# A spectral filter and a SiLU network on one core: rows of a transfer over more ports, loads of d2 two pieces ahead, roundings of the ramp at other places

## The chip, the cores and the metric

The kernel runs on one core of a Trainium2 chip. The metric is device time in microseconds (us) of one execution. Before the change it is 2659.55 us, the median of three runs (2658.20 to 2661.21).

A core has a matrix engine (TensorE, PE in the profile, with its weight loads as PEld), a vector engine (VectorE, DVE), a scalar engine (ScalarE, ACT), a general one (GpSimd, POOL), and SyncE (SP), which does nothing but issue transfers and wait. ACT and POOL issue transfers too. All transfers are moved by the core's 16 DMA engines. Each engine works through its own list of instructions in order and waits on semaphores where it needs another's result. SBUF is the on-chip memory of 128 partitions that engines and transfers use; PSUM holds the results of matmuls.

## What is computed

Two blocks, one after the other. The first filters a sequence in the frequency domain; the second is a small network on every token.

```python
# x: (8, 3008, 256), filt_r and filt_i: (1505, 256)
X = np.fft.rfft(x, axis=1)
F = (filt_r + 1j * filt_i)[None, :, :]
y = np.fft.irfft(X * F, n=x.shape[1], axis=1)
t = y.reshape(8 * 3008, 256)
h = t @ w_in                        # (256, 2048), given in float64
g = h * (1.0 / (1.0 + np.exp(-h)))
out = g @ w_out                     # (2048, 256), given in float64
```

## The kernel before

**The network.** It is the larger part. The 24064 tokens are cut into 48 pairs of chunks (`PAIRS`: two chunks of 256, 256 or 240 tokens), six pairs to one of the eight batch entries, here called blocks. A pair takes eight steps, one for each two slices of 128 hidden units, so a block has `STEPS` = 48 steps. In a step, `hidden` computes h and SiLU and `project`, one step behind, multiplies by w_out. Both products are done in seven instead of eight block products (the names A11, S1 to S4 and so on), which costs additions on DVE and POOL. A step has eight rounds (`ROUNDS`); after each one, pieces of other work whose due time has come are emitted. A due time is a step and a round, and `put(step, round, piece)` notes it. The order written out this way is the order in every engine's list.

**The filter.** The transform of length 3008 = 47 x 64 is done as matmuls in two stages, once forward and once back, with a pass through DRAM between the stages to exchange rows and columns:

- `load_x` brings pieces u = 0 to 7 of a block's input into SBUF. Of the 128 partitions, rows 0 to 46 (h = 0) and 64 to 110 (h = 1) are filled. A piece is loaded by four transfers: for each h one of 32 rows and one of 15. Blocks 0 and 1 use it for all pieces, the later ones for pieces 6 and 7 alone (the others come by `load_fold`). In block 0 even pieces are issued by SP and odd ones by ACT, and the unused rows 32 to 63 are zeroed first by a memset (L271), which the transfers that touch rows from 32 on wait for. `sums` (L291) adds and subtracts the two halves of the piece on DVE.
- `stage1` is the first matmul stage (L308). Its results are copied out by `evac`, which takes DVE and ACT by turns, and are written to d1 in DRAM from POOL (L313).
- `load_t2(g)` reads d1 back for groups g = 0 to 5 (L382). `forward` (L393) multiplies, `multiply` (L405) applies the filter on DVE, `add` (L413, L414) finishes the complex product, on POOL in block 0 and on DVE later.
- `inverse` (L426), `even` (L437) and `rows` (L445, L450) do the first stage back and write d2 in DRAM.
- `load_t4(g)` reads d2 for g = 0 to 7 (L455, two transfers on SP, into two buffers by turns). `stage3(g)` (L458) issues the load of piece g + 1, does 64 small matmuls (L469) and copies the result into y, the input of the network. In the steady part a block's pieces 0 to 3 are due 11, 9, 6 and 3 steps before the block's first step, pieces 4 to 7 at 10 3/8, 11 3/8, 16 3/8 and 18 6/8.

The filters stay in SBUF. `load_filters` (L219) fetches them in two parts, rows 0 to 3 of each partition (groups 0 and 1) and rows 4 to 11 (groups 2 to 5). Each part is 16 transfers, and each of these fills 16 neighbouring partitions: which frequency a partition holds follows from `kept`, from which the tables of the transform are built too.

**The weights.** They come as float64, and `load_weights` fetches the raw words of two slices by four transfers on SP. `round_weights(j)` makes float32 of slice j: five operations on DVE (L722 to L730), two on ACT, two products on POOL (L735), and after every second slice four more additions on POOL (`combine_weights`, L551).

**The ramp.** Before step 0 block 0 must go through the filter, and some weights must be there. The list at the end of the kernel sets that order: x loads, d_t, weights(0), first filters, `sums` and `stage1`, load_t2(0) and (1), e_t, rounded(0) and (1). Then for each group: forward; in group 0 the second filters, wi_t and wq_t; weights(1 + g) for g < 3; multiply and add; a rounding of slice g for g = 2, 3 and 4; and inverse_rows of the group before. After the last group come weights(4), load_t4(0), the roundings 5 to 8 (weights(5) after the first) and stage3(0) to (3). Then the steps begin, with the roundings 9 to 15 and block 1's x pieces 0 to 7 in their rounds; the x pieces 0 and 1 of block 1 and the first `tokens` and `sums` are due just before step 0.

**Transfers on SP and ACT** take eight completion semaphores by turns, as the kernel is built: the one that takes a semaphore waits until the transfer that had it before has landed. So at most eight transfers of the two are in flight. Those from POOL have eight of their own.

Of the kernel before, what the change touches and what calls it, by code (L numbers as in the profile page):

```python
# [52 lines left out]
B, S, C = 8, 3008, 256  # L53
DFF = 2048
N1, N2 = 47, 64
NS, NG = 24, 6
# [18 lines left out]
def slot_residue(g, bank, j):  # L75

    s = 2 * g + bank
    return (s, 47 - s, s + 12, 35 - s)[j]
# [6 lines left out]

def kept(sp):

    r = np.arange(32)
    return np.where(r < 16, sp + 94 * r, 94 * (r - 15) - sp)


def dft_tables():
# [63 lines left out]
def kernel(  # L156
# [47 lines left out]
    f_t = [cpool.tile([128, NG, 2, C], FP32, name=f"filt{i}") for i in range(2)]  # L204
# [5 lines left out]
    x_t = [x_all[:, i] for i in range(2)]  # L210

    def load_filters(first, last):
        for j in range(4):
            s0, tau = slot_residue(0, 0, j), (1 if j % 2 == 0 else -1)
            for half in range(2):
                off, t = (s0, tau) if half == 0 else (94 - s0, -tau)
                for k, filt in enumerate((filt_r, filt_i)):
                    p0 = 32 * j + 16 * half
                    nc.sync.dma_start(  # L219
                        out=f_t[k][p0:p0 + 16].rearrange("p g k c -> p (g k) c")[:, first:last],  # L220
                        in_=bass.AP(tensor=filt.tensor, offset=filt.offset + (off + t * first) * C,
                                    ap=[[94 * C, 16], [t * C, last - first], [1, C]]))

# [12 lines left out]
    def bank(b, name, spare=None):  # L236


        if b > 0 and spare is not None:
            return accps.tile([128, 2, C], FP32, name=name, tag=f"a{spare}")  # L240
        if b > 0 or early[0] is None:
            return fps.tile([128, 2, C], FP32, name=name, tag="f")
        early[0] += 1
        k = early[0] % 6
        if k < 2:
            return fps.tile([128, 2, C], FP32, name=name, tag="f")
        return accps.tile([128, 2, C], FP32, name=name, tag=f"a{k - 2}")

    def spectral(b):
# [3 lines left out]
        xs, us, t2s, banks, prods, halves, t4s = {}, {}, {}, {}, {}, {}, {}  # L253

        def load_x(u):


            queue = nc.sync
            if b == 0:
                queue = (nc.sync, nc.scalar)[u % 2]  # L260
                if u == 0:
                    us["t1"] = gpool.tile([128, 2, 2, 2, C], FP32, name="t1_g", tag="g")
                if u in (0, 2):
                    xs["y"] = ypool.tile([128, 2, HALF], FP32, name=f"x_{b}_{u}", tag="y")
                if u < 4:
                    xs[u] = xs["y"][:, u % 2, 0:1024].rearrange("p (a n) -> p a n", a=2)
                elif u < 6:
                    xs[u] = t4pool.tile([128, 2, 2 * C], FP32, name=f"x_{b}_{u}", tag="t4")
                else:
                    xs[u] = x_t[u % 2]  # L270
                (nc.vector, nc.gpsimd)[u % 2].memset(xs[u][32:64], 0.0)  # L271
            else:
                xs[u] = x_t[u % 2]
            for h in range(2):
                for r0, nr in ((0, 32), (32, N1 - 32)):
                    queue.dma_start(
                        out=xs[u][64 * h + r0:64 * h + r0 + nr],
                        in_=bass.AP(tensor=x.tensor,
                                    offset=x.offset + (b * S + 32 * r0 + 4 * u + 2 * h) * C,
                                    ap=[[32 * C, nr], [32 * N1 * C, 2], [1, 2 * C]]))  # L280

        def sums(u):
            if b > 0 or u % 3 == 0:
# [168 lines left out]
        def load_t4(g):  # L452
            t4s[g] = t4pool.tile([128, 4, C], FP32, name=f"t4_{b}_{g}", tag="t4")
            for h in range(2):
                nc.sync.dma_start(out=t4s[g][64 * h:64 * h + 2 * NS],  # L455
                                  in_=d2[:, 4 * g:4 * g + 4, h, :])

        def stage3(g):  # L458
            half, n0 = divmod(4 * g, 16)
            if g < 7:  # L460
                load_t4(g + 1)
            ps = [bank(b, f"pd_{b}_{g}_{h}").rearrange("p a c -> p (a c)")[:, 0:8 * N1]
                  .rearrange("p (a i n) -> p a i n", a=2, i=4) for h in range(2)]
            for cb in range(2):
                for i in range(4):
                    for c0 in (0, 64):
                        for h in range(2):
                            rows = slice(64 * h, 64 * h + 2 * NS)
                            nc.tensor.matmul(  # L469
                                out=ps[h][c0:c0 + 64, cb, i, :],  # L470
                                lhsT=t4s[g][rows, i, 128 * cb + c0:128 * cb + c0 + 64],
                                rhs=wi_t[rows, :], start=True, stop=True)
            if n0 == 0:
                y[b, half] = ypool.tile([128, 2, HALF], FP32, name=f"y_{b}_{half}", tag="y")
            dst = y[b, half].rearrange("p a (r h n) -> p a h n r", h=2, n=16)
            for h in range(2):
                evac(dst[:, :, h, n0:n0 + 4], ps[h])
# [7 lines left out]
    def put(step, rnd, piece, *args):  # L485

        pending.append((step + rnd / ROUNDS, len(pending), lambda: piece(*args)))

    def plan(b, part):

        at = STEPS * b
# [37 lines left out]
        for g, step in ((0, -32), (2, -24), (4, -16)):  # L529
# [3 lines left out]
            put(at + step + 1, 5, part["rows"], g, 0, 2)  # L533
            put(at + step + 2, 3, part["rows"], g, 1, 2)
        put(at - 14, 5, part["load_t4"], 0)
        for g, step in enumerate((-11, -9, -6, -3)):
            put(at + step, 3, part["stage3"], g)
        plan_rest(b, part)
# [219 lines left out]
    def weights(jp):  # L758
        if wide:
            load_weights(jp)  # L760

    def rounded(j):
        if wide:
            round_weights(j)
        else:
            load_exact(j)

    def inverse_rows(part, g):
        part["inverse"](g)
        for i in range(2):  # L770
            part["even"](g, i)
            part["rows"](g, i)
# [5 lines left out]
    part = spectral(0)  # L778
# [16 lines left out]
    for g in range(NG):  # L795
        part["forward"](g)
        if g == 0:
            load_filters(4, 2 * NG)
            nc.sync.dma_start(out=wi_t, in_=wi_dram.ap())
            nc.sync.dma_start(out=wq_t, in_=wq_dram.ap())  # L800
        if g < 3:
            weights(1 + g)
        for k in range(2):
            part["multiply"](g, k)
        for k in range(2):
            part["add"](g, k)
        if 2 <= g < NG - 1:
            rounded(g)
        if g > 0:
            inverse_rows(part, g - 1)  # L810
    inverse_rows(part, NG - 1)
    weights(4)
    part["load_t4"](0)
    for j in range(5, 9):
        rounded(j)
        if j == 5:
            weights(5)
# [4 lines left out]
    for b in range(1, B):  # L822
        plan(b, spectral(b))
# [67 lines left out]
```

## Time and profile before

The profiled execution took 2658.93 us, of which the span from the first to the last instruction is 2657.1. The profile shows for each engine when it worked and what ended its idle time.

| stretch (us) | what it is | PE busy | DVE busy | DMA share | GB/s |
|---|---|---|---|---|---|
| 0 to 20 | x loads, first stage | 11.93 | 14.61 | 0.71 | 198 |
| 20 to 40 | weights(0), first filters, d1 | 7.15 | 10.14 | 0.95 | 316 |
| 40 to 60 | groups 0 and 1, second filters | 8.11 | 6.66 | 0.96 | 182 |
| 60 to 80 | groups 2 and 3 | 7.86 | 14.33 | 1.03 | 249 |
| 80 to 100 | groups 4 and 5 | 15.28 | 16.40 | 0.54 | 165 |
| 100 to 130 | roundings 5 to 8, stage3, first step | 14.39 | 23.58 | 0.67 | 158 |
| 130 to 160 | first steps | 27.98 | 24.54 | 0.35 | 99 |
| 320 to 600 | steady part, for comparison | 279.89 | 187.05 | 0.28 | 69 |

"Busy" is the time in which the engine worked within the stretch, "DMA share" the mean busy share of the 16 DMA engines (a little over 1 where the records of packets overlap), and GB/s what they moved. A wait in a timeline stands in square brackets behind an instruction: how long its engine was idle before it and what ended that.

The first step's first matmul starts at 122.66 us. The clock that TensorE was granted is 1.00 until about 53 us, 0.50 from there to about 135 us, and 1.00 again from then on but for one stretch of 3.4 us near 222 us. Over the whole span PE is busy 97% of the time, DVE 65%, ACT 41% and POOL 18%.

### The profile page before, as it was taken

The numbers are of one execution on the slowest core, as the hardware profiler recorded it, in microseconds if no ns is written. First come the engines' busy times: TensorE is split into PE (matmuls) and PEld (weight loads), VectorE is DVE, ScalarE is ACT, GpSimd is POOL, SyncE is SP. The second block draws the span as 40 slices with busy tenths as digits, with TensorE's granted clock in tenths as the row PEclk, the third lists the DMA queues.
The fourth block names the chain that finished last, engine by engine and source line by source line (L and its number), as shares of the span: only waits on it lengthen the run. The fifth ranks groups of instructions, "written<-read, shape, count | busy, mean of one in ns | idle before, by whom it ended". The sixth has DMA issues, their size and how long they took to land.

```text
span 2657.1 us, 48172 instructions
## 1 busy us (share of the span) xinstructions
PE 2566.0 (97%) x18720; PEld 2166.4 (82%) x18720; DVE 1728.3 (65%) x3590; ACT 1095.7 (41%) x3000; POOL 484.1 (18%) x726
## 2 busy tenths in 40 slices
PE   4689999999999999999999999999999999999998
PEld 1368888888887888888888888888888788888987
DVE  5786766667666666666666676666766666555554
ACT  1244444443444444444444444444444444444443
POOL 4541111311121112112111211131112111100100
PEclk9599999999999999999999999999999999999999
DMA  8632221232223222231222322123222321111000
GB/s 229 176 103 64 75 67 45 70 78 71 50 72 80 55 63 73 69 70 48 75 64 56 70 75 67 44 70 77 71 50 72 79 56 28 48 22 27 9 16 16
DMA packets 206379, 176.11 MB, mean 66 GB/s; under 512 B 122916, under 2 KB 177956, under 8 KB 205748
## 3 DMA queue, kind: packets, MB, share of 16 engines
q1 hardware_dynamic: 185184, 120.90, 19.9%
q0 software_dynamic: 17296, 47.47, 5.6%
q10 hardware_dynamic: 3672, 4.67, 0.6%
q8 instruction: 147, 2.41, 0.4%
q14 instruction: 80, 0.66, 0.1%
HBM read 97.97 MB, written 84.41 MB: 69 GB/s over the span
## 4 chain that ended last, share of the span: by engine, by line
PE 90%; DMA 3%; DVE 3%; SPq 1%; issue 1%; ACT 1%; POOL 0%; ACTq 0%; DVEq 0%; POOLq 0%
PE acc L639 41%; PE px L580 25%; PE pyz L580 18%; PE pd L469 2%; DMA t<-d 2%; PE pb L393 2%; PE pc L426 2%; DVE g L551 1%; SPq L677 1%; PE pf L363 1%; PE pa L308 1%; DVE u L291 0%; DMA x<-in_x_dram 0%; DMA filt<-in_filt_r_dram 0%; DMA e_t<-e_tbl 0%
## 5 line engine op out<-in xcount | busy, mean ns | idle before, releaser
L639 PE MATMUL acc<-g,w_t 128*128 128x256 f32 (+1 forms) x5376 | 1513.8, 375 | 0.4 <-DVE g L551 0.4
L639 PEld LDWEIGHTS acc<-g,w_t 128*128 128x128 f32 x5376 | 1022.5, 190 | 116.1 <-DVE g L551 0.8
L551 DVE TENSOR_TENSOR g<-pyz,abc 128x256 f32<-128x256 f32 (+1 forms) x1152 | 480.0, 417 | 536.7 <-ACT abc L601 294.6
L551 DVE TENSOR_TENSOR g<-g 128x256 f32<-128x256 f32 (+3 forms) x1152 | 619.7, 538 | 196.7 <-ACT g L584 183.5
L580 PE MATMUL px<-ty,w_t 128*128 128x256 f32 (+1 forms) x2304 | 688.6, 381 | 3.5 <-ACT abc L595 3.0
L584 ACT ACTIVATE g<-g 128x256 f32<-128x256 f32 (+1 forms) x1152 | 473.0, 411 | 247.6 <-DVE g L551 247.5
L551 POOL TENSOR_TENSOR s<-s 128x256 f32<-128x256 f32 (+1 forms) x329 | 259.8, 806 | 1461.1 <-DVE s L657 1450.1
L580 PEld LDWEIGHTS px<-ty,w_t 128*128 128x128 f32 x2304 | 425.0, 190 | 88.5 <-issue 30.7
L580 PE MATMUL pyz<-y,w_t 128*128 128x256 f32 (+1 forms) x1536 | 454.7, 378 | 1.9 <-DVE g L551 1.9
L580 PEld LDWEIGHTS pyz<-y,w_t 128*128 128x128 f32 x1536 | 284.1, 190 | 48.4 <-DVE g L551 6.6
L595 ACT COPY abc<-px 128x256 f32<-128x256 f32 (+1 forms) x384 | 141.3, 368 | 365.8 <-PE px L580 365.8
L584 ACT ACTIVATE g<-px 128x256 f32<-128x256 f32 (+1 forms) x384 | 145.8, 380 | 308.8 <-PE px L580 308.8
L601 ACT COPY abc<-px 128x256 f32<-128x256 f32 (+1 forms) x384 | 143.7, 374 | 311.4 <-PE px L580 311.2
L580 PE MATMUL px<-y,w_t 128*128 128x256 f32 (+1 forms) x768 | 230.2, 382 | 3.6 <-ACT g L584 2.6
L580 PE MATMUL pyz<-ty,w_t 128*128 128x256 f32 (+1 forms) x768 | 225.9, 376 | 0.7 <-DVE g L551 0.7
L580 PEld LDWEIGHTS px<-y,w_t 128*128 128x128 f32 x768 | 142.1, 190 | 43.0 <-ACT g L584 15.4
L580 PEld LDWEIGHTS pyz<-ty,w_t 128*128 128x128 f32 x768 | 145.7, 190 | 18.6 <-DVE g L551 2.3
L588 ACT COPY abc<-px 128x256 f32<-128x256 f32 (+1 forms) x384 | 135.0, 352 | 2.7 <-PE px L580 1.3
L229 DVE COPY y<-pd 128x376 f32<-128x376 f32 x64 | 51.1, 804 | 112.2 <-PE pd L469 112.2
L469 PEld LDWEIGHTS pd<-wi_t,t 48*64 48x64 f32 x4096 | 71.2, 140 | 45.3 <-issue 32.3
L469 PE MATMUL pd<-wi_t,t 48*64 48x47 f32 x4096 | 80.3, 239 | 23.4 <-DMA t<-d 15.3
L393 PE MATMUL pb<-t,d_t 64*32 64x256 f32 x1536 | 61.7, 408 | 36.7 <-DMA t<-d 36.7
(67 smaller groups left out, 1346.0 us busy)
## 6 DMA issues: line engine op xcount, KB each, us to landing
t<-d SPq DMA_DIRECT2D x96, 256.0 KB
t<-d SPq DMA_DIRECT2D x128, 192.0 KB
d<-q POOLq DMA_DIRECT2D x85, 256.0 KB, 2.6
out_dram<-o SPq DMA_DIRECT2D x636, 32.0 KB
d<-tf POOLq DMA_DIRECT2D x144, 96.0 KB, 2.5
d<-t POOLq DMA_DIRECT2D x52, 192.0 KB, 3.1
xr<-in_x_dram SPq DMA_DIRECT2D x6, 1472.0 KB
x_all<-in_x_dram SPq DMA_DIRECT2D x72, 96.0 KB
```

Source lines behind the costliest of these rows:

```text
L229: nc.vector.tensor_copy(out=dst, in_=src)
L308: nc.tensor.matmul(out=ps[h][64 * par:64 * par + 64], lhsT=wf_t[rows, par], rhs=ut[rows, par], start=True, stop=True)
L393: nc.tensor.matmul(out=ps[k][32 * j:32 * j + 32, ri, :], lhsT=d_t[rows, 4 * g + at, ri, :], rhs=t2[rows, at, :], start=True, stop=True)
L426: nc.tensor.matmul(out=ps[j][64 * k:64 * k + 64, a, :], lhsT=e_t[rows, g + a, k, ri, :], rhs=zs[k][rows, ri, :], start=(a == 0 and ri == 0 ...
L469: nc.tensor.matmul(out=ps[h][c0:c0 + 64, cb, i, :], lhsT=t4s[g][rows, i, 128 * cb + c0:128 * cb + c0 + 64], rhs=wi_t[rows, :], start=True, ...
L551: eng.tensor_tensor(out=out, in0=in0, in1=in1, op=op)
L580: nc.tensor.matmul(out=out, lhsT=w_t[:, c, 0, jp], rhs=rhs, start=start, stop=True, skip_group_check=True)
L584: nc.scalar.activation(out=g[:, k, 0:n], in_=g[:, k, 0:n] if src is None else src, func=AFT.Silu)
L588: nc.scalar.copy(out=sums[:, 0, 0:n], in_=xo)
L595: nc.scalar.copy(out=sums[:, 1, 0:n], in_=xo)
L601: nc.scalar.copy(out=sums[:, 2, 0:n], in_=xo)
L639: nc.tensor.matmul(out=acc[pair][i][:, h, 0:n], lhsT=w_t[:, c, 1, jp], rhs=g[:, k, 0:n], start=(jp == 0 and h == 0), stop=last, skip_group ...
```

## The change

It has four parts.

- **Filters.** `kept` puts the frequencies of a residue on even partitions and those of its mirror on odd ones, where they were on the first and second 16 of a block of 32. So a filter transfer fills 16 partitions two apart, spread over 32, instead of 16 neighbours. The blocks of 32 are loaded in the order 0, 2, 1, 3. The tables follow `kept` by themselves; sizes and the number of transfers stay.
- **x rows.** A piece's 47 rows of one h are loaded by three transfers of 16, 16 and 15 rows that are three apart, instead of one of 32 and one of 15. Six transfers per piece instead of four. Each next transfer goes to the other h; odd pieces begin with h = 1. All transfers with h = 0 now touch rows from 32 on.
- **Loads of d2.** load_t4(1) is issued with load_t4(0), and stage3(g) issues load_t4(g + 2) after its matmuls instead of load_t4(g + 1) before them.
- **Roundings of the ramp.** Slices 2 and 3 are rounded after group 1, that is before group 2 is multiplied; slice 4 after the last group with 5 to 8. Before, slices 2, 3 and 4 were rounded within groups 2, 3 and 4.

```diff
 def kept(sp):
-    r = np.arange(32)
-    return np.where(r < 16, sp + 94 * r, 94 * (r - 15) - sp)
+    r = np.arange(32) // 2
+    return np.where(np.arange(32) % 2 == 0, sp + 94 * r, 94 * (r + 1) - sp)
...
     def load_filters(first, last):
-        for j in range(4):
+        for j in (0, 2, 1, 3):
...
-                    p0 = 32 * j + 16 * half
                     nc.sync.dma_start(
-                        out=f_t[k][p0:p0 + 16].rearrange("p g k c -> p (g k) c")[:, first:last],
+                        out=f_t[k][32 * j + half:32 * j + 32:2].rearrange("p g k c -> p (g k) c")[:, first:last],
...
-            for h in range(2):
-                for r0, nr in ((0, 32), (32, N1 - 32)):
+            for r0 in range(3):
+                for h in (range(2) if u % 2 == 0 else (1, 0)):
                     queue.dma_start(
-                        out=xs[u][64 * h + r0:64 * h + r0 + nr],
+                        out=xs[u][64 * h + r0:64 * h + N1:3],
                         in_=bass.AP(tensor=x.tensor,
                                     offset=x.offset + (b * S + 32 * r0 + 4 * u + 2 * h) * C,
-                                    ap=[[32 * C, nr], [32 * N1 * C, 2], [1, 2 * C]]))
+                                    ap=[[3 * 32 * C, (N1 + 2 - r0) // 3], [32 * N1 * C, 2], [1, 2 * C]]))
...
         def stage3(g):
-            if g < 7:
-                load_t4(g + 1)
...
+            if g < 6:
+                load_t4(g + 2)
...
         put(at - 14, 5, part["load_t4"], 0)
+        put(at - 14, 5, part["load_t4"], 1)
...
-        if 2 <= g < NG - 1:
-            rounded(g)
         if g > 0:
             inverse_rows(part, g - 1)
+        if g == 1:
+            rounded(2)
+            rounded(3)
     inverse_rows(part, NG - 1)
     weights(4)
     part["load_t4"](0)
-    for j in range(5, 9):
+    part["load_t4"](1)
+    for j in range(4, 9):
         rounded(j)
```

## Prediction, made before the changed kernel was run

> **What bounds the kernel now.** I read the page's busy shares first, then the windows over three stretches, then the waits, and last the timelines of the places that the waits name. The windows:
>
> ```profile
> 0.00:130.00 130.00, 64.71 (x715) 29.49 (x716) 85.71 (x140) 27.64 (x50) 60.39 (x85) 0.70 0.80 207
> 130.00:190.00 60.00, 52.95 (x236) 36.84 (x236) 51.19 (x93) 26.68 (x66) 29.96 (x41) 0.96 0.38 107
> 190.00:2657.00 2467.00, 2448.34 (x17771) 2100.06 (x17770) 1591.38 (x3358) 1041.42 (x2884) 393.78 (x601) 1.00 0.23 58
> ```
>
> From 190 us on the matmuls are busy for 2448 of 2467 us: TensorE sets the end, and only what leaves it idle can be won. The first 125 us, the ramp, are another kernel: PE is half idle, and the transfers (share 0.80) and the order on DVE set the pace. In the steady part one wait is left (the waits of PE, 190 us to the end):
>
> ```profile
> PE pd L469 <- DMA t<-d: 7.8, 12, 1.2
> ```
>
> Its place, in the timeline of the first block:
>
> ```profile
> 210.69 4.93 SPq L677 DMA_DIRECT2D out_dram<-o  x8
> ...
> 215.72 0.87 SPq L455 DMA_DIRECT2D t<-d  x2
> ...
> 219.02 0.28 PE L469 MATMUL pd<-wi_t,t 48*64 48x47 f32 x2 [1.04 <-DMA t<-d]
> 219.78 1.47 PE L469 MATMUL pd<-wi_t,t 48*64 48x47 f32 x62 [0.48 <-DMA t<-d]
> ```
>
> The load for stage3(5) stands on SP behind eight output stores and lands after PE wants it. The same happens once in each of the eight blocks. In the ramp the long wait is DVE's for the filters of groups 2 to 5, with the weights' rounding behind it:
>
> ```profile
> 63.63 0.69 DVE L405 TENSOR_TENSOR z<-pb,filt 128x512 f32<-128x512 f32 x1 [13.95 <-DMA filt<-in_filt_r_dram]
> ...
> 66.60 0.43 DVE L722 TENSOR_SCALAR work<-raw 128x512 uint32<-128x512 uint32 x1 [0.24 <-DMA raw<-in_moe_w_out_dram]
> ```
>
> and in the windows of that stretch the engines of the DMA are full while little moves:
>
> ```profile
> 52.00:56.00 4.00, 0.00 (x0) 0.00 (x0) 0.00 (x0) 0.00 (x0) 0.00 (x0) 0.65 0.66 137
> 56.00:60.00 4.00, 0.00 (x0) 0.00 (x0) 0.00 (x0) 0.00 (x0) 0.00 (x0) 0.50 1.16 121
> 60.00:64.00 4.00, 0.00 (x0) 0.00 (x0) 0.37 (x1) 0.00 (x0) 0.00 (x0) 0.50 1.09 113
> ```
>
> **What the Trainium skill says.** "SBUF — State Buffer", section Door 1: the port of a partition follows from its number; 16 neighbouring partitions reach 4 ports (104 GB/s), 32 reach 8 (189 GB/s), and +64 goes to the other eight. The trace agrees with the first: 113 to 121 GB/s at a full share above. "DMA: Bandwidth & Descriptors", anatomy of one DMA: some 2 us of each transfer do not depend on its size. Agrees: the page has 2.5 us to landing for 96 KB of tf and 2.6 for 256 KB of q; the first x transfers take 2.2 to 3.2 from issue to their last completion update. "TensorE: Matmul & The Clock Gate", part 1: an idle stretch halves the clock in steps of 3.4 us. Agrees: after the gap at 218 us the granted clock is 0.50 from 220.4 for 3.4 us. "SBUF — State Buffer", who interferes with whom: tensor_scalar and GpSimd lock each other out. Agrees: L724 takes 0.42 us alone and 0.95 beside POOL.
>
> **Steady part: d2's loads two ahead.** load_t4(5) now goes out after stage3(3), 13 steps before its use, instead of at stage3(4), one step before. Take the time from the start of the last matmul before a stage3 piece to the first after it: 1.39 us where nothing waits; in the eight stage3(5) 3.57, 1.80, 3.25, 2.02, 2.86, 2.08, 3.47, 2.92. Sum 21.97 - 8 x 1.39 = 10.85 us. In the first block the clock is also lost for 3.4 us at half: 1.7. Together 12.5 us off PE, which is the bound there. What is late next: the load behind the stores at step 10 is now load_t4(6), used 6 steps (some 40 us) later: nothing. New wait: SP now holds each load until stage3(g) has read the buffer; behind it stand stores and prefetches used steps later. Nothing, at most 1 us over the run. The twelve x transfers of pieces 6 and 7 per block instead of eight (0.4 us each on SP) are needed 1.6 steps later: nothing.
>
> **Ramp, x loads.** 32 transfers of 128 and 60 KB become 48 of 64 or 60. SP and ACT take eight completion semaphores in turn, so a transfer waits for the one eight before (the waits of SP, 0 to 20 us):
>
> ```profile
> SPq L276 <- DMA x<-in_x_dram: 5.8, 8, 1.3
> ```
>
> Before: last issue at 15.31, (15.31 - 0.91) / 31 = 0.46 us each, a life of 8 x 0.46 = 3.7. The ports of a whole half (47 rows) do not change; alternating halves relieve them. I take a life of 2.9 (between 2.3 alone and 3.7): 0.36 each, last issue 0.9 + 47 x 0.36 = 17.8, 2.5 later, and ACT's first eviction, which waits 13.57 us behind its issues, with it. Row 0 also waits for the memset on SP, 0.9 us. The first filters run faster behind it, so I take +1.5 us at load_t2(0) (ends -2 and +4).
>
> **Ramp, filters.** Sixteen transfers of 128 KB, first issue 42.46. The chain shows the last issued at 56.53 and landing 7.81 later, 64.34; the last eight landed about 1.1 us apart. On eight ports I take 0.55 us (ends 0.45 and 0.8; 189 GB/s of the page gives 0.68 as an estimate, alternating halves less). The first cannot land before t2(2), 48.9 + 1.5 = 50.4, so the last lands at 50.4 + 15 x 0.55 = 58.7, not 64.3.
>
> **Ramp, roundings.** Now rounded(2) and (3) stand before multiply(2) on DVE and need raw(1), which is behind the filters on SP. Before, raw's first half came 2.2 us after the filters (66.51 against 64.34): 60.9. One rounding with POOL free is 2.9 us (99.47 to 102.36), with POOL busy 4.4 (106.72 to 111.19); I take 6.5 for both: multiply(2) starts at 67.4, not 63.63. Then three roundings are gone from between the groups: 66.6-70.0, 75.64-79.33, 84.2-88.38, 11.3 us of the 35.9 from 63.63 to the last rows (99.56), which leaves 24.6. But on POOL the additions of group 2 now stand behind rounded(3)'s products and combine (1.4 + 2.9, up to 6): inverse(2) and rows(2) wait some 2.8 more. Rows end at 67.4 + 24.6 + 2.8 = 94.8. The tail has five roundings instead of four: 2.9 + 4 x 4.4 = 20.5 (before 16.1), end 115.3, as against 115.65. After it, before, PE waited for its loads:
>
> ```profile
> 118.69 0.41 PE L469 MATMUL pd<-wi_t,t 48*64 48x47 f32 x2 [2.98 <-DMA t<-d]
> 119.74 1.95 PE L469 MATMUL pd<-wi_t,t 48*64 48x47 f32 x62 [0.64 <-DMA t<-d]
> ...
> 124.54 1.28 DVE L291 TENSOR_TENSOR u<-x_all 111x512 f32<-111x512 f32 x2
> 125.74 0.42 DVE L551 TENSOR_TENSOR g<-pyz,abc 128x256 f32<-128x256 f32 x1
> ```
>
> With loads two ahead stage3(3) waits only for its banks: one eviction (0.8) and 2.0 us of matmuls, done at 118.1 instead of 121.7. But load_t4(5) now waits on SP for those matmuls, and block 1's first x loads stand behind it: 0.9 us of issue for load_t4(5), 2.6 for six x transfers, 2.8 to land: 124.4, where DVE could take them at 121. So u runs 124.4 to 125.6, and g at 125.6 against 125.74. Sum of the ramp: -0.1 us. The filters' gain is paid to the x loads, to POOL's order and to this wait. Ends: filters 0.45, no x loss and no POOL delay -6; filters 0.8 and +4 in front +6.
>
> **Sum.** -12.5 - 0.1 and 0.6 for small SP waits: -12.0. The profiled execution took 2658.93 (span 2657.1), so 2646.9; it lies 0.62 below the median 2659.55, which gives 2647.5.
>
> **Rivals.** (1) As summed, 0.62: 2643.5 to 2651.5. (2) The spread pays in full, the x of block 1 comes in time, 0.15: ramp -6, 2641.5. For it: 0.5 us per transfer is within what 16 engines moved at 24 to 32 us (around 400 GB/s); against: raw(1) still comes last. (3) More, smaller x transfers keep their life of 3.7 (48 x 0.46 = 22 instead of 15 us), 0.15: ramp +7.5, 2655. For it: the eight in flight. Half of it is within 0.2%. (4) Slower, 0.08: transfers to partitions two or three apart are themselves slower than to neighbours. Place: the second filters. The time to g is the filters' landing + 66.9, so the loss eats the 12.5 when they land at 71.3: (71.3 - 50.4) / 15 = 1.4 us per transfer, against 1.1 before. At 2.0 it would be +9, 2668. No row of this trace has such a stride; against it, each row stays a run of 1 to 8 KB. (5) That stage3(5) still waits: the order on SP excludes it.
>
> **Chances.** What a measurement of this kernel tells from no change is 0.2%, 5.3 us. Faster: cases 1 and 2 and a third of 3, 0.82; same 0.11; slower 0.07. The range 2640 to 2657 leaves out case 4 and the edges of 2 and 3, under 0.2.
>
> **What would show it.** PE's wait for t<-d after 190 us gone and no half clock at 220; eight stage3(5) at 1.39 us; the windows between 46 and 60 us at about 200 GB/s; multiply(2) on DVE after two roundings near 67, g's first addition near 125; a wait of u for x_all just before it. I am wrong if the filters land after 62, if ACT's first eviction starts past 20, or if DVE's waits for raw grow beyond the filters' gain.

## The result, and the profile after

The changed kernel takes 2660.26 us (median of four runs, 2659.17 to 2661.77); the kernel before took 2658.88 beside it. The ratio is 1.0005, with a 95% interval of 0.9988 to 1.0022: no change that can be measured. The forecast was 2647.5, so 12 us of gain are missing. The profiled execution of the changed kernel took 2659.17 us with a span of 2657.4 (before: 2658.93 and 2657.1).

The windows of the changed kernel over the three stretches of the prediction (columns: stretch, its length, busy us of PE, PEld, DVE, ACT and POOL with the number of instructions, granted clock, DMA share, GB/s):

```profile
0.00:130.00 130.00, 56.87 (x710) 26.56 (x710) 79.22 (x131) 25.26 (x45) 58.05 (x83) 0.76 0.72 204
130.00:190.00 60.00, 48.94 (x213) 33.52 (x214) 50.33 (x91) 25.59 (x64) 29.93 (x40) 0.90 0.41 114
190.00:2657.00 2467.00, 2453.15 (x17798) 2102.80 (x17797) 1595.45 (x3369) 1045.41 (x2892) 394.67 (x603) 1.00 0.23 58
```

In the first 190 us PE is busy 11.9 us less than before (105.8 against 117.7): the ramp has become longer. After 190 us it is busy for 2453 us instead of 2448, with 27 matmuls more. That is work left over from the late ramp, not a better filled engine. The waits of PE after 190 us say why the steady part won so little (engine, tile and line, what it waited for: us in total, times, longest):

```profile
PE pb L394 <- DMA t<-d: 3.5, 6, 1.1
```

Before, the tile here was pd (stage3), with 7.8 us. That wait is gone, and forward, which waited nowhere after 190 us before, has taken its place. The time from the last matmul ahead of a piece to the first after it counts more than the wait itself, since it holds the whole stall. Over 1.33 us, which a forward takes without a wait, the seven forward(0) of blocks 1 to 7 lose 1.78, 0.14, 2.10, 1.17, 0, 0.96 and 0.22: 6.36 us.

The place, a block after the one that the prediction showed. First the timeline of SP in the changed kernel (start, length, queue, line, operation, out<-in, how many):

```profile
853.73 4.58 SPq L679 DMA_DIRECT2D out_dram<-o  x8
858.66 2.71 SPq L383 DMA_DIRECT2D t<-d  x4
```

and that of PE in the same kernel:

```profile
854.73 1.15 PE L468 MATMUL pd<-wi_t,t 48*64 48x47 f32 x64
...
862.45 0.59 PE L394 MATMUL pb<-t,d_t 64*32 64x256 f32 x2 [0.31 <-DMA t<-d]
864.17 1.09 PE L394 MATMUL pb<-t,d_t 64*32 64x256 f32 x30 [1.13 <-DMA t<-d]
```

The same place in the kernel before, SP and then PE:

```profile
853.62 3.30 SPq L382 DMA_DIRECT2D t<-d  x4
```

```profile
851.61 0.28 PE L469 MATMUL pd<-wi_t,t 48*64 48x47 f32 x2 [0.93 <-DMA t<-d]
852.48 1.14 PE L469 MATMUL pd<-wi_t,t 48*64 48x47 f32 x62 [0.59 <-DMA t<-d]
859.82 1.09 PE L393 MATMUL pb<-t,d_t 64*32 64x256 f32 x32
```

In step 10 of a block, results are stored by two groups of eight transfers. The load for stage3(5) stood on SP behind the first eight, and the load for forward(0) stands behind all 16. Before, it landed at 858.49 (last completion update of load_t2(0)'s two transfers) and PE came at 859.82: 1.3 us of slack, because PE had just lost 1.9 us at stage3(5). In the changed kernel PE no longer loses them, while the load lands 5.5 us after its issue: 864.13. Seen from PE's step, the loads behind the stores are no earlier than before, and PE meets them one piece later.

The ramp, by when steps start (first of the 14 matmuls of `hidden` in the step), and the sum over the whole span:

| | before | after | difference |
|---|---|---|---|
| step 0 | 122.66 | 124.84 | +2.2 |
| step 1 | 131.62 | 138.19 | +6.6 |
| step 6 | 177.69 | 183.65 | +6.0 |
| stage3(5), eight places, over 1.39 us | 10.85 | 0 | -10.85 |
| clock at half near 222 us (in step 11) | 1.3 | 0 | -1.3 |
| forward(0), seven places, over 1.33 us | 0 | 6.36 | +6.36 |
| step 6 and the three rows below it, added | | | +0.2 |
| span | 2657.1 | 2657.4 | +0.3 |

The clock's share is worked out from the difference to before, which falls from +6.01 at the start of step 11 to +2.53 at the start of step 12: 3.48, of which 2.18 are that block's stage3(5). This share isn't shown to be the change's. All six kernels below that keep the old loads of d2 (e4, e7, e8, e9, e11 and e12) wait at the same stage3(5) and still have the full clock there. In the kernel before, PE waited 1.04 and 0.48 us, and this window follows (the clock is the third number from the end):

```profile
220.40:223.80 3.40, 3.40 (x41) 2.86 (x33) 1.76 (x3) 1.18 (x2) 0.00 (x0) 0.50 0.57 134
```

In e7 PE waited longer, and the clock stayed at 1.00:

```profile
224.31 0.28 PE L469 MATMUL pd<-wi_t,t 48*64 48x47 f32 x2 [1.39 <-DMA t<-d]
225.11 1.14 PE L469 MATMUL pd<-wi_t,t 48*64 48x47 f32 x62 [0.52 <-DMA t<-d]
```

```profile
224.00:228.00 4.00, 3.17 (x72) 2.82 (x73) 1.42 (x3) 1.02 (x2) 0.00 (x0) 1.00 0.47 94
228.00:232.00 4.00, 4.00 (x20) 3.42 (x19) 3.31 (x8) 2.06 (x6) 0.00 (x0) 1.00 0.98 244
```

So the 10.85 us at stage3(5) did go away where they were expected to. More than half of them (6.36) came back one piece later on PE, and the ramp cost about as much again.

How the ramp became longer. First ACT's first eviction in the kernel before:

```profile
15.80 1.56 ACT L231 COPY t<-pa 128x512 f32<-128x512 f32 x3 [13.57 <-DMA x_all<-in_x_dram]
```

ACT in the changed kernel, its own x transfers and its first eviction:

```profile
9.49 7.63 ACTq L277 DMA_DIRECT2D x<-in_x_dram  x10
17.16 4.49 ACTq L277 DMA_DIRECT2D x_all<-in_x_dram  x6
21.69 1.56 ACT L231 COPY t<-pa 128x512 f32<-128x512 f32 x3 [19.46 <-DMA x_all<-in_x_dram]
```

ACT can copy nothing out before its 24 x transfers are issued, at 0.75 us each in these rows; the eviction starts at 21.69 instead of 15.80. DVE in the changed kernel, at the rounding of slice 2, at multiply(2) and at the first sum of block 1:

```profile
70.05 0.43 DVE L724 TENSOR_SCALAR work<-raw 128x512 uint32<-128x512 uint32 x1 [14.64 <-DMA raw<-in_moe_w_out_dram]
...
76.34 0.68 DVE L406 TENSOR_TENSOR z<-pb,filt 128x512 f32<-128x512 f32 x1
...
131.09 1.29 DVE L292 TENSOR_TENSOR u<-x_all 111x512 f32<-111x512 f32 x2 [4.65 <-DMA x_all<-in_x_dram]
132.30 0.42 DVE L553 TENSOR_TENSOR g<-pyz,abc 128x256 f32<-128x256 f32 x1
```

multiply(2) starts 12.7 us later than before. It no longer stands behind the filters alone but behind raw(1), which SP fetches after them, and two roundings. At the end of the ramp u waits 4.65 us for block 1's x, which the prediction had as a new wait, and the first g comes at 132.30 instead of 125.74. SP in the changed kernel shows what that x stands behind:

```profile
110.50 14.24 SPq L456 DMA_DIRECT2D t<-d  x8
124.78 13.46 SPq L277 DMA_DIRECT2D x_all<-in_x_dram  x18
```

The last of these eight transfers belong to load_t4(5), which goes out only after stage3(3).

The second filters, by SP in the changed kernel:

```profile
53.95 0.62 SPq L219 DMA_DIRECT2D filt<-in_filt_r_dram  x1
56.78 0.60 SPq L219 DMA_DIRECT2D filt<-in_filt_i_dram  x1
57.42 1.19 SPq L219 DMA_DIRECT2D filt<-in_filt_r_dram  x1
59.79 0.58 SPq L219 DMA_DIRECT2D filt<-in_filt_i_dram  x1
```

Each issue costs about 0.6 us or more, and SP stood still from 54.6 to 56.8 and from 58.6 to 59.8 (the end of one row to the start of the next). The sixteen took 18.2 us from the first issue to the last landing (48.86 to 67.02), instead of 21.9 before (42.46 to 64.35): faster as such, but they start 6.4 us later.

### The profile page after: what moved, and what is told of

It reads as the page before. It is cut to its first block, busy times and chain, and to the rows that moved or that the text cites. A ratio compares the mean times of both kernels' runs of the same rounds, so it can differ in the third digit from the quotient of the medians.

```text
span 2657.4 us, 48231 instructions
## 1 busy us (share of the span) xinstructions
PE 2559.0 (96%) x18720; PEld 2162.9 (81%) x18720; DVE 1725.0 (65%) x3590; ACT 1096.3 (41%) x3000; POOL 482.7 (18%) x726
## 4 chain that ended last, share of the span: by engine, by line
PE 92%; DVE 2%; SPq 2%; DMA 2%; issue 1%; ACT 0%; POOL 0%; DVEq 0%; ACTq 0%; POOLq 0%
PE acc L641 42%; PE px L582 25%; PE pyz L582 18%; PE pd L468 2%; PE pb L394 2%; PE pc L427 2%; SPq L277 1%; DMA t<-d 1%; PE pf L364 1%; PE pa L309 1%; DMA raw<-in_moe_w_out_dram 0%; SPq L219 0%; DVE g L553 0%; DVE u L292 0%; SPq L679 0%
```

## The experiments

Runs of one kernel lie several us apart: the kernel before, beside the experiments, ran from 2654 to 2665 with medians of 2658.23, 2658.14 and 2657.92. So times are compared by the ratio to the runs of before that were taken beside them. A profile is of one execution, which can lie off the median too: those of e2 and e4 took 2.7 and 4.2 us longer than their medians, those of e7 and e11 1.9 and 4.0 less. The start of the ramp varies from run to run as well. The kernel before and e6 (below) have the same list up to load_t2(0), which was issued at 33.96 in the one profile and at 36.73 in the other; for e9 and e10, which also agree up to there, it was 33.84 and 36.45. A difference of 2 or 3 us in one ramp is therefore not an effect by itself.

### One part undone at a time

e1 is the changed kernel with the four x transfers of before.

```diff
-            for r0 in range(3):
-                for h in (range(2) if u % 2 == 0 else (1, 0)):
+            for h in range(2):
+                for r0, nr in ((0, 32), (32, N1 - 32)):
```

> The changed kernel with x loaded by four transfers of neighbouring rows, as before. Theory A (the issue of a transfer whose partitions are two or three apart holds SP or ACT 0.6 us or more where one to neighbours holds it 0.35; so the x phase is set by issue): ACT's first eviction comes 5 us earlier than in the changed kernel, and the first x pieces of block 1 land some 2 us earlier behind load_t4(5); step 1 starts about 6 us earlier, the time is 2653 to 2655. Theory B (the roundings' place or the filters' transfers made the ramp longer, x is hidden by what follows): less than 2 us earlier at step 1, 2658 or more.

Measured: 2653.32 us, ratio 0.9983 (0.9975 to 0.9990); by the ratios that is 5.8 us below the changed kernel. The delay runs through the ramp nearly undiminished:

| us | before | after | e1 | after minus e1 |
|---|---|---|---|---|
| last x issue | 15.31 | 20.76 | 15.20 | 5.6 |
| first eviction on ACT | 15.80 | 21.69 | 15.58 | 6.1 |
| load_t2(0) issued | 33.96 | 40.39 | 34.70 | 5.7 |
| second filters, first issue | 42.46 | 48.86 | 42.87 | 6.0 |
| second filters, last landing | 64.35 | 67.02 | 59.15 | 7.9 |
| multiply(2) | 63.63 | 76.34 | 67.87 | 8.5 |
| last rows | 99.56 | 101.57 | 93.10 | 8.5 |
| step 1 | 131.62 | 138.19 | 129.54 | 8.7 |

DVE in e1, at the rounding of slice 2 and at multiply(2):

```profile
61.53 0.43 DVE L723 TENSOR_SCALAR work<-raw 128x512 uint32<-128x512 uint32 x1 [12.10 <-DMA raw<-in_moe_w_out_dram]
...
67.87 0.68 DVE L405 TENSOR_TENSOR z<-pb,filt 128x512 f32<-128x512 f32 x1
```

With x as before, the ramp is the one that the prediction worked out (67.4 for multiply(2), 94.8 for the last rows), and its step 1 comes 2.1 us before that of the kernel before, which is within the spread of one ramp. The x loads alone made the ramp's loss. The span of e1 is 5.1 below that of before. The ramp gives 2.1 of that at step 1. In the steady part 12.15 us of stage3(5) and clock are set against 7.2 us that forward(0) waits here, which leaves 4.95. Behind the last of these waits e1 then runs at half clock for 3.4 us from 2118.3, and its lead over before falls by 1.7 us there. Together that is 5.4.

e2 is the changed kernel with `kept` and the filter transfers of before.

```diff
-    r = np.arange(32) // 2
-    return np.where(np.arange(32) % 2 == 0, sp + 94 * r, 94 * (r + 1) - sp)
+    r = np.arange(32)
+    return np.where(r < 16, sp + 94 * r, 94 * (r - 15) - sp)
...
-        for j in (0, 2, 1, 3):
+        for j in range(4):
...
-                        out=f_t[k][32 * j + half:32 * j + 32:2].rearrange("p g k c -> p (g k) c")[:, first:last],
+                        out=f_t[k][p0:p0 + 16].rearrange("p g k c -> p (g k) c")[:, first:last],
```

> The changed kernel with the filters on 16 neighbouring partitions and blocks in order 0 to 3, as before. Theory A: the filters are cheaper to issue (0.4 instead of 0.6 us each) but limited by four ports again; the second filters take 21 to 22 us from first issue to last landing instead of 18.2, the ramp is 2 to 4 us longer, the time 2662 to 2664. Rival: the dearer issue costs what the ports give, and the time stays within 1 us of the changed kernel's 2660.

Measured: 2660.62 us, ratio 1.0010 (1.0004 to 1.0017), against 1.0005 (0.9988 to 1.0022) with the spread filters: not told apart by time, as its rival had it. Its profile has the filters in 23.2 us instead of 18.2 (48.30 to 71.46), multiply(2) 3.2 later and step 1 3.2 later, and a span of 2661.5, 4.1 longer. That the spread shortens the loading is shown: the second filters take 16.3 to 18.2 us in the profiles of all five kernels with spread filters, and 20.8 to 23.2 in those of the nine without. That the ramp gains by it is not shown.

e3 is the changed kernel with the roundings at their places of before.

```diff
+        if 2 <= g < NG - 1:
+            rounded(g)
         if g > 0:
             inverse_rows(part, g - 1)
-        if g == 1:
-            rounded(2)
-            rounded(3)
...
-    for j in range(4, 9):
+    for j in range(5, 9):
```

> The changed kernel with the roundings 2, 3 and 4 within groups 2, 3 and 4, as before. Theory A: multiply(2) starts when the second filters land, near 67 us, instead of at 76.3, and the three roundings (11 us) come back between the groups; DVE's idle time before it falls from 14.6 to 11 us, and stage3(3) waits for its load again; step 1 comes 0 to 4 us earlier, time 2656 to 2660. Theory B (the place of the roundings is what made the ramp longer): step 1 comes 6 us or more earlier, time 2654 or less.

Measured: 2654.89 us, ratio 0.9987 (0.9981 to 0.9994): 4.8 us below the changed kernel by the ratios, whose intervals just overlap. It lies between the two theories. multiply(2) starts at 65.97, just as the filters land (66.14), instead of 76.34. The last rows are no earlier (102.36 against 101.57), since three roundings stand between the groups again, but the tail has one rounding less and step 1 comes at 135.60, 2.6 earlier, again within the spread of one ramp. Another 2.2 us are forward(0)'s, which loses 4.18 here instead of 6.36; why it loses less in this run isn't settled. Over the kernels that have the new loads of d2 and the old place of load_t2 this sum was 4.18, 4.76, 6.36, 6.58 and 7.2.

e4 is the changed kernel with the d2 loads of before.

```diff
         def stage3(g):
+            if g < 7:
+                load_t4(g + 1)
...
-            if g < 6:
-                load_t4(g + 2)
...
-        put(at - 14, 5, part["load_t4"], 1)
...
-    part["load_t4"](1)
```

> The changed kernel with d2's loads one piece ahead, as before. Theory C (the loads two ahead took 12 us of waits from stage3(5), and of these 6.4 came back as waits of forward(0) for load_t2(0), and 4.4 as the wait of block 1's first sums for x behind load_t4(5)): the waits at stage3(5) are back, those at forward(0) gone, step 1 comes 3 to 4 us earlier; the time is 2661 to 2663, within 3 us of the changed kernel. Rival (nothing was given back, the loads are worth the 12 us of the forecast): 2671 to 2673.

Measured: 2661.74 us, ratio 1.0015 (1.0008 to 1.0021), which isn't told from the changed kernel; the rival's 2671 is out. PE's waits after 190 us in e4:

```profile
PE pd L470 <- DMA t<-d: 8.9, 13, 1.5
```

stage3(5) loses 11.82 us again, and forward(0) nothing. So one wait is exchanged for the other; step 1 comes at 135.31, 2.9 earlier than in the changed kernel. The way from step 0 to step 1 takes 8.7 us instead of 13.3, since block 1's x no longer stands behind load_t4(5). The d2 loads win in the steady part and pay in the ramp.

### One part alone

The roundings were not run alone. e5 is the kernel before with the new loads of d2 alone, so the edit is e4's turned round.

> The kernel before with d2's loads two pieces ahead and nothing else. Theory C: the 10.85 us of waits at stage3(5) and some 1.3 us of half clock go, about 6.4 us come back at forward(0) waiting for load_t2(0), and block 1's first x, behind load_t4(5), costs 3 to 4 us at step 1. Sum -2 to -3: 2655 to 2657. Rival (the forecast's step): nothing comes back, 2646 to 2647.

Measured: 2653.62 us, ratio 0.9985 (0.9979 to 0.9992), 4.5 us below before and a little more than theory C had. PE's waits after 190 us in e5:

```profile
PE pb L393 <- DMA t<-d: 2.0, 4, 0.8
```

No wait for pd, and forward(0) loses 4.76. In the profile: -10.85 - 1.3 + 4.76, and +1.1 at step 1, where block 1's first x are issued at 119.71 instead of 116.61, make -6.3; its span is 6.2 shorter than before. The sum closes with this part and the clock near 222 us, which, as said, isn't shown to be this part's.

e6 is e5 with two more edits, one for each thing that gave the gain back. The loads for forward(0) and forward(1) go out between the two groups of eight stores instead of after them (step 10, round 4 instead of step 11, round 0), and block 0's load_t4(5) goes behind block 1's first x.

```diff
+            if g < 6 and (b, g) != (0, 3):
+                load_t4(g + 2)
...
-        put(at - 37, 0, part["load_t2"], 0)
-        put(at - 37, 0, part["load_t2"], 1)
+        put(at - 38, 4, part["load_t2"], 0)
+        put(at - 38, 4, part["load_t2"], 1)
...
     plan_rest(0, part)
+    put(2, 3, part["load_t4"], 5)
```

> As e5, with load_t2(0) and (1) half a step earlier, before the second eight output stores, and in block 0 load_t4(5) after block 1's first x loads. Theory C: both places that gave the gain back are freed, forward(0) waits no more, step 1 comes when it did in the kernel before; the time is 12 us under before, 2645 to 2648. Rival: SP has too little room at step 10, and the wait moves on once more (to the loads of group 2, or the stores hold up DVE's transposes), 2650 to 2655.

Measured: 2647.66 us (2647.50 to 2647.99), ratio 0.9964 (0.9952 to 0.9977): faster than both kernels, by 10.5 us than before. The same place in SP's timeline of e6, then PE's:

```profile
846.35 2.68 SPq L382 DMA_DIRECT2D t<-d  x4
849.13 6.33 SPq L678 DMA_DIRECT2D out_dram<-o  x8
```

```profile
847.65 1.15 PE L467 MATMUL pd<-wi_t,t 48*64 48x47 f32 x64
854.99 1.09 PE L393 MATMUL pb<-t,d_t 64*32 64x256 f32 x32
```

load_t2(0) is issued before the second stores and lands at 851.86, 3.1 us before PE wants it; neither piece has a bracket. PE's waits for t<-d after 190 us are gone altogether. The span is 11.2 us shorter than before: 12.15 won in the steady part, the clock's 1.3 among them, and 1.5 lost at step 1 (133.10), of which 0.6 is made up by step 8. The steady gain of the prediction was there to be had, with load_t2 ahead of the second stores. What the other edit adds wasn't run apart: from step 0 to step 1 it takes 10.7 us in e6, 13.0 in e5 and 9.0 before.

e8 is the kernel before with the spread filters alone, the edit being e2's turned round.

> The kernel before with the filters over eight ports and nothing else. Theory A: issue at 0.6 to 0.7 us each is what limits them now, not the ports; the second filters take about 16.5 us from first issue to last landing (before 21.9; the forecast's 0.55 us each would make it 13.5), multiply(2) starts near 60 instead of 63.6, step 1 is 2 to 4 us earlier: 2654 to 2656. Rival: the forecast's step, landing by 57, 2652 or less; or nothing gained, 2658.

Measured: 2655.91 us, ratio 0.9994 (0.9986 to 1.0002): 2 us at most likely, and not told from none. The second filters take 17.2 us (46.75 to 63.99) instead of 21.9, but they began 4.3 later in this execution, and multiply(2) is where it was (63.77), not near 60. Whether the first filters' dearer issues caused the late start isn't settled: in e1 the issues of the same first filters end at 34.4, 0.7 after those of before. In e8 the first of them already went out 1.7 us later than before.

### What it is about the x loads

e7 is the kernel before with six x transfers per piece, of the changed kernel's sizes, but of neighbouring rows.

```diff
-            for h in range(2):
-                for r0, nr in ((0, 32), (32, N1 - 32)):
+            for r0, nr in ((0, 16), (16, 16), (32, N1 - 32)):
+                for h in (range(2) if u % 2 == 0 else (1, 0)):
```

> The kernel before with x loaded by six transfers per piece of 16, 16 and 15 neighbouring rows, in the changed kernel's order of h. Same count and sizes as the changed kernel, without the stride. Theory A (the stride of the partitions makes the issue dear): mean issue 0.35 to 0.45 us, last issue of the 48 at 15.5 to 17.5 us, ACT's first eviction near 16 to 18. Rival (more and smaller transfers as such, at most eight in flight): issue as in the changed kernel or lives of 2.6 us set the pace anyway, last issue near 20.7, first eviction near 21.7, the ramp 4 us longer.

e11 is the kernel before with the changed x loads alone, so it differs from e7 in the step between the rows, in SBUF and in DRAM.

> The kernel before with the changed x loads alone (six transfers per piece, every third row). Against e7 (six transfers per piece of neighbouring rows) only the step between the partitions differs. Theory A (the strided transfer's dearer issue comes on top of the count): mean issue 0.7 us, last x issue at 20.5 to 21 us (e7: 19.4), first eviction at 21.7 (e7: 19.8), time 2662 to 2666. Theory B (spreading over ports wins back what the issue costs): last issue at 19.4 or earlier, eviction at or below 19.8, time at or below e7's 2664.

Measured: e7 2663.95 us, ratio 1.0022 (1.0013 to 1.0032); e11 2664.67 us, ratio 1.0025 (1.0015 to 1.0036).

| x transfers | before | e7 | e11 | after |
|---|---|---|---|---|
| number | 32 | 48 | 48 | 48 |
| mean issue on SP or ACT | 0.37 | 0.36 | 0.72 | 0.72 |
| mean life, issue to last completion update | 3.53 | 3.14 | 2.64 | 2.67 |
| last issue | 15.31 | 19.42 | 20.76 | 20.76 |
| first eviction on ACT | 15.80 | 19.80 | 21.69 | 21.69 |

Here are SP's waits in the first 20 us, of e7 and then of the changed kernel:

```profile
SPq L276 <- DMA x<-in_x_dram: 8.0, 13, 1.2
```

```profile
SPq L277 <- DVE x L271: 1.0, 1, 1.0
SPq L879 <- PEq L879: 0.7, 1, 0.7
SPq L277 <- DVE u L292: 0.3, 1, 0.3
```

The two kernels are limited by different things and come out alike. e7 is held by the eight in flight: 3.14 / 8 = 0.39 us from one issue to the next, which is also (19.42 - 0.9) / 47. Its cheap issue, as theory A had it, brings no early end. In the changed kernel no x transfer waits for an earlier one at all. Two queues at 0.72 us an issue have become the limit: 0.36 us from one issue to the next, and (20.76 - 0.91) / 47 = 0.42 with the start, where ACT's second issue comes only at 3.72, when POOL's memset of its rows has ended (3.69). Lives are 0.5 us shorter than e7's, but fewer transfers are in flight (2.67 / 0.42 = 6.4 on average instead of 8), so how much of that the spread itself does isn't shown. The larger number costs 4.1 us at the last issue, the step between rows 1.3 more there and 1.9 at the eviction. In the total the second can't be seen: the intervals of e7 and e11 nearly coincide. All of x is worth 6.8 us put in (e11) and, by the ratios, 5.8 taken out (e1).

e12 is the kernel before with its own four transfers in another order, the two halves in turn.

```diff
-            for h in range(2):
-                for r0, nr in ((0, 32), (32, N1 - 32)):
+            for r0, nr in ((0, 32), (32, N1 - 32)):
+                for h in (range(2) if u % 2 == 0 else (1, 0)):
```

> The kernel before with its own four x transfers per piece, of neighbouring rows, but in another order: the 32-row transfers of both halves first, then the 15-row ones, and the halves change places in every second piece. Theory A (transfers in flight at once on the same ports hold one another up): the life of an x transfer falls from 3.7 to below 3.4 us, the last issue comes at 14 us or before (before: 15.3), the first eviction 1 us earlier. Theory B (the count in flight and the bytes set the pace): lives of 3.6 to 3.8, last issue at 15 to 15.6, no change in time.

Measured: 2658.28 us, ratio 1.0002 (0.9994 to 1.0011). Lives 3.53 as before, last issue 14.24, eviction 14.36: between the two theories. The life doesn't fall, and yet 1.1 us is won at the issue. load_t2(0) is issued at 34.34 none the less (before: 33.96), so in this profile nothing of it reached the spectra. A gain of 1 us with x can't be seen in the time, while 5.5 us lost there cost about as much.

### The filters by order alone

e9 is the kernel before with the filter transfers in another order, so that four in a row go to four groups of partitions.

```diff
-        for j in range(4):
-            s0, tau = slot_residue(0, 0, j), (1 if j % 2 == 0 else -1)
-            for half in range(2):
-                off, t = (s0, tau) if half == 0 else (94 - s0, -tau)
-                for k, filt in enumerate((filt_r, filt_i)):
+        for j0 in (0, 1):
+            for k, half, j in [(k, half, j) for k in range(2) for half in range(2) for j in (j0, j0 + 2)]:
+                    s0, tau = slot_residue(0, 0, j), (1 if j % 2 == 0 else -1)
+                    off, t = (s0, tau) if half == 0 else (94 - s0, -tau)
+                    filt = (filt_r, filt_i)[k]
```

> The kernel before with one edit: the filter transfers keep their 16 neighbouring partitions and their bytes, but are issued in another order, so that four consecutive ones go to four different groups of partitions instead of four to the same group. The issue cost on the engine should then stay near 0.4 us, where the strided transfers of the changed kernel cost 0.8. Theory A (what limits the filters is that the transfers in flight together sit on the same few ports): the second filters' loads, 21.9 us from first issue to last landing in the kernel before, shorten to 16.5 us or less, the first product with a second filter starts at 58 to 60 us instead of 63.6, and the time is 2653 to 2655 us, 3 to 5 below before. Theory B (the ports are not the limit; what counts is the data moved beside the spectra's loads and the number of transfers in flight): 21 to 22 us, product at 63 to 64 us, 2657 to 2659.

Measured: 2657.13 us, ratio 0.9995 (0.9987 to 1.0004). The windows of e9 over the second filters, and those of e1, where the filters are spread:

```profile
52.00:56.00 4.00, 1.08 (x32) 0.54 (x16) 0.00 (x0) 0.00 (x0) 0.00 (x0) 1.00 0.79 171
56.00:60.00 4.00, 0.00 (x0) 0.00 (x0) 0.00 (x0) 0.00 (x0) 0.00 (x0) 0.50 1.09 135
```

```profile
52.00:56.00 4.00, 0.00 (x0) 0.00 (x0) 0.00 (x0) 0.00 (x0) 0.00 (x0) 0.66 0.65 191
56.00:60.00 4.00, 0.00 (x0) 0.00 (x0) 0.00 (x0) 0.00 (x0) 0.00 (x0) 0.50 0.67 186
```

The order doesn't replace the spread. The sixteen take 22.0 us, with the DMA engines fully busy again (1.09) at 135 GB/s, against 186 to 191 at a share of 0.66 in e1. Their issue has a mean of 0.46 us (before 0.40). Theory A falls. multiply(2) did start at 60.43, since the real filters, which it waits for, now come ahead of the imaginary ones within each pair of groups, but no gain can be told in the time.

e10 is e6 with e9's order, both edits as shown.

> The kernel of e6 (d2's loads two ahead, the two spectra loads of the following block ahead of the second stores, the sixth d2 load of block 0 behind the x of block 1), with the filters' issue order of e9. Theory A: the two gains add, 2643 to 2645 us, with no wait for d2 and none for the spectra at the first forward transform. Theory B: the filters' order gives nothing, and the time is that of e6, 2647 to 2648.

Measured: 2645.78 us (2642.70 to 2646.79), ratio 0.9956 (0.9944 to 0.9968). It has the lowest median of all the kernels run, but its interval overlaps e6's by more than half, and e9 showed no effect of the order. What can be said is that both are 10 to 12 us faster than before. Theory A's 2643 to 2645 is just missed.

## Why the prediction was wrong, point by point

- **Steady part, the wait removed: right.** The eight stage3(5) came down to 1.39 us each, which is the 10.85 us forecast. The half clock near 220 us, forecast at 1.7 us, is gone too and measured 1.3, since 0.3 of it already stood in the sum of stage3(5) (its last 62 matmuls took 1.47 us at half clock, e7's 1.14). That is luck as much as foresight, since six other kernels have the wait and not the half clock there. The wait on SP for stage3(g) and the twelve x transfers per block cost nothing that a trace shows. Rival (5) is out.
- **"What is late next: the load behind the stores at step 10 is now load_t4(6), used 6 steps later: nothing": wrong, 6.4 us.** This is the first failed step. It looked at the next load of the same kind. The next load on the queue was load_t2(0), with 1.3 us of slack, and PE was about to arrive 1.9 us earlier. e5 shows the wait with this part alone, e6 shows that it goes when the loads stand ahead of the second stores.
- **Ramp, x loads: the second failed step, 5.5 us for 2.5.** Taken were a life of 2.9 and thus 0.36 us per transfer. The life fell further than that, to 2.67, but not for the reason given, that alternating halves relieve the ports: e12 alternates them with the transfers of before, and the life stays at 3.53. And the life no longer mattered. The spacing was set by the issue, priced at nothing, which doubled to 0.72 us: 0.42 us per transfer, last issue 20.76 instead of 17.8. e7 shows that more transfers would have been late even with the cheap issue (19.42, a life of 3.14). And nothing behind it made up for the delay, where "+1.5 at load_t2(0)" was taken: it was 6.4 in this execution and 5.7 against e1, above the upper end of 4. Rival (3) has the size (22 us, +7.5) but not the reason, since it kept the life at 3.7.
- **Ramp, filters: right in direction, the size too small.** From the first landing to the last, the fifteen later transfers took 0.87 us each in the changed kernel ((67.02 - 53.93) / 15), 0.78 in e8 and 0.73 in e1, against 1.01 before and 0.55 forecast. In "SBUF — State Buffer", Door 1, the Trainium skill gives 189 GB/s for eight ports, from which the prediction had worked out an estimate of 0.68 and then set it aside for less. The 186 to 191 GB/s that all transfers together moved in e1's windows are of that size, and 0.68 would have been the nearer guess for all three. That the ports set the pace there isn't shown: the DMA share was 0.65 to 0.67, and an issue took 0.6 us itself. In e1 the last landing is 59.15 against the 58.7 forecast, but only because its first landing came 2 us before the start assumed.
- **Ramp, roundings: the sequence right, shifted by x.** In e1 multiply(2) starts at 67.87 (67.4 forecast) and the last rows end at 93.10 (94.8). In the changed kernel the two are 8.9 and 6.8 late. Whether the cost of putting raw(1) ahead of group 2 was judged too low is open. With x late, undoing it gained 4.8 us by the ratios (e3), at the edge of what these can tell, with 2.6 at step 1.
- **Ramp, the end: right.** u waits for block 1's x behind load_t4(5) and starts 10.0 us after the roundings end (9.1 forecast), and stage3(3) is done 2.8 us after them, as forecast. All of it came 6 to 7 us late, so the ramp's sum was +6.0 instead of -0.1.
- **The sum.** -12.0 was forecast. The table of the result gives -10.85 - 1.3 + 6.36 + 6.0. Two terms of about 6 us were missing, and each alone would have left half the gain.

Of the signs at the prediction's end, the three conditions for being wrong are met: filters after 62 us (67.02), an eviction past 20 (21.69), and a wait of DVE for raw that grew (from 0.24 to 14.64 us before the rounding of slice 2) while the filters landed no earlier than before.

## What to carry to other kernels

When a stall on the bounding engine goes, everything after it on that engine comes earlier by its length. So list the next few loads on the same queue with their slack in the trace, of whatever kind they are, before writing "nothing". Splitting a transfer, or striding it over partitions, can be paid on the engine that issues it. Multiply the number by the issue time over the queues that issue, as well as by life over the number in flight, and take the larger. Where a part of a change gives back another's gain, test the parts alone: here the d2 loads with two small edits in the order (e6) gave 10.5 us without the three others.

## What the runs showed of the hardware that was not expected

- The issue of a transfer on SP and ACT depends on the partitions it goes to. For x it took a mean of 0.36 us with neighbouring rows (e7) and 0.72 with every third row (e11), at the same count and sizes; there the rows are also further apart in DRAM. With the filters only the SBUF side differs. The second sixteen took a mean of 0.39 to 0.46 us in the nine kernels with neighbours and 0.59 to 0.68 in the five with partitions two apart. The first sixteen don't separate as well, with 0.50 to 0.91 and 0.75 to 0.98. Two single ones of them, in e1 (two apart) and in e6 (neighbours):

```profile
33.15 0.59 SPq L219 DMA_DIRECT2D filt<-in_filt_r_dram  x1
```

```profile
35.52 0.42 SPq L219 DMA_DIRECT2D filt<-in_filt_r_dram  x1
```

  What on the issuing side makes the difference no run here shows.
- Interleaving transfers to different groups of partitions in the order of issue did not have the effect of spreading each one: 22.0 and 20.8 us for the sixteen filters (e9, e10) against 16.3 to 18.2. No run here shows why.
- Smaller transfers have shorter lives, but not in proportion: with eight in flight, 64 and 60 KB took 3.14 us (e7), where 128 and 60 KB took 3.53 (before). With the number in flight fixed, splitting them lowered what was moved per us: the last x transfer was issued at 19.42 instead of 15.31.
- The length of a wait of PE did not decide alone whether the clock fell to half after it. After waits of 1.04 and 0.48 us near 219, the kernel before ran at 0.50 for 3.4 us; after waits of 1.39 and 0.52 us near 224, e7 kept 1.00.
